# Decode attention kernel: all transposes and scores of a tile first, then its softmax chain between parts of the value product of the tile before

## The chip, the cores and the metric

The kernel runs on one core of one Trainium2 chip. The metric is the device time of one execution in microseconds (us), medians of several runs.

## The reference

One decode step of attention with a cache, times a gate that a small MLP computes. What matters is the attention: 4 batches times 8 K/V heads, 8192 cached positions of 256 numbers in bf16, two query heads for each K/V head.

```python
B, Sq, D = 4, 1, 448
Hq, Hkv, Sk, Dh = 16, 8, 8192, 256
...
q = (x @ wq).reshape(B, Sq, Hq, Dh).transpose(0, 2, 1, 3)
k = repeat(k_cache, 2, axis=1); v = repeat(v_cache, 2, axis=1)
scores = einsum("bhqd,bhkd->bhqk", q, k) * (Dh ** -0.5)
o = einsum("bhqk,bhkd->bhqd", softmax(scores), v)
...            # output projection, times the gate, plus x
```

There are 32 pairs of batch and K/V head. The kernel calls each a tile (`h` = 0 to 31). A tile has 4 MiB of K and 4 MiB of V, each used once: 268 MB in all.

## The kernel before

K and V have two buffers each (`h % 2`). For each tile TensorE transposes K in 16 groups of 8 blocks (`f_t`); VectorE and ScalarE copy each group from PSUM to SBUF; TensorE multiplies it with the query (`f_s`, three groups behind: `LAG`). Then comes the softmax chain: row maxima (VectorE), their transpose on TensorE (`f_rmaxT`), global maximum (VectorE), broadcast by a matmul (`f_bc`), exponentials (ScalarE), sum by a matmul (`f_sum`). Last is the value product (`f_pv`, 128 matmuls).

```python
    J_RMAX, J_BC, J_SUM = 4, 6, 9
    PV_SLOTS = tuple(range(10, 16))
...
            def load_k(h):                       # issued by SyncE, K buffer free again
                if h >= 2:
                    sp.wait_ge(S["p_t"], NGR * (h - 1))
...
            def load_v(h):                       # V buffer free: value product of h-2 done
                    sp.wait_ge(S["p_pv"], h)
...
            for h in range(2, NH):
                load_k(h)
                load_v(h - 1)
            load_v(NH - 1)
...
            def body(h):                         # TensorE; NGR = 16
                for j in range(NGR):
                    f_t(h, j)
                    if j >= LAG:
                        f_s(h, j - LAG)
                    else:
                        f_s(h - 1, NGR + j - LAG)
                    if j == J_RMAX:
                        f_rmaxT(h - 1)
                    if j == J_BC:
                        f_bc(h - 1)
                    if j == J_SUM:
                        f_sum(h - 1)
                    if j in PV_SLOTS:
                        i, n = PV_SLOTS.index(j), len(PV_SLOTS)
                        f_pv(h - 1, NPV * i // n, NPV * (i + 1) // n)

            with nc.Fori(0, NH // 2, ...):       # a loop on TensorE: 2 bodies, 16 times
                body(0)
                body(1)

            h = NH - 1                           # after the last body
            for j in range(NGR - LAG, NGR):
                f_s(h, j)
...
            for g in range(0, 3):                # output product of 7 groups of heads,
                f_o(g)                           # with tile 31's chain between its parts
            f_rmaxT(h)
            for g in range(3, 6):
                f_o(g)
            f_bc(h)
            for g in range(6, HKV - 1):
                f_o(g)
            f_sum(h)
            # ... value product of tile 31 in four pieces, last group of the output product
```

So a body holds the last three score groups and the whole chain of the tile before it.

## Time and profile before

| | before |
|---|---|
| median time | 665.11 us (664.92 to 665.47, 3 runs) |
| loads | 279 MB, 431 GB/s from 40 to 640 us |
| TensorE idle until K is there | 93.9 us, 30 times |
| first transpose of the first tile, of the last tile | 31.26, 635.92 us |
| result stored from | 660.93 us |

The page of the profile. The rows of digits are 40 slices of the span, in tenths, 9 for 90% and more.

```profile
span 663.0 us, 27886 instructions
...
PE   2388887789888878987887898888888887789777
...
PEclk9997888898877899888789987878998788899889
DMA  8999999999999999999999999999999999999993
```

The DMA row is full from the second slice to the last but one. TensorE is not, and its granted clock is below full in most slices. The table of windows gives the busy time of each engine in a stretch, then clock, DMA share and GB/s:

```profile
40.00:640.00 600.00, 499.38 (x11974) 493.53 (x11972) 220.94 (x491) 235.04 (x336) 5.59 (x30) 0.87 1.01 431
...
635.00:641.00 6.00, 5.08 (x88) 5.09 (x89) 2.07 (x4) 2.05 (x2) 0.00 (x0) 0.72 0.98 422
...
650.00:652.00 2.00, 2.00 (x70) 2.00 (x67) 1.12 (x2) 0.24 (x1) 0.00 (x0) 1.00 0.66 274
652.00:654.00 2.00, 2.00 (x112) 1.75 (x112) 0.99 (x5) 0.00 (x0) 0.00 (x0) 1.00 0.12 49
```

The loads run without a gap until about 651 us and then stop. What follows is not bound by loads. The view of waits (in total, times, longest, in us) shows what TensorE stands idle for:

```profile
PE pst L484 <- PEq L436: 93.9, 30, 8.1
```

L484 is the transposes; the wait ends when the K of the tile has landed, 3 us per body. So the loop goes at the pace of the loads. The timeline of the end (start, duration, engine, line, operation, and in brackets the idle time before it):

```profile
635.92 0.61 PE L484 MATMUL pst<-ident_b,kn 128*128 128x128 bf16 x8 [3.11 <-PEq L436]
...
645.67 0.68 PE L522 MATMUL psv<-pT,vb 128*128 128x32 bf16 x21 [0.41 <-PEq L436]
...
655.90 0.36 PE L514 MATMUL psm<-rowsum,ones_f 128*128 128x2 f32 x2 [0.78 <-PEq L436]
...
660.93 0.63 SPq L160 DMA_DIRECT2D out_dram<-out_b  x2
```

The last K is there at 635.92 us, and from then TensorE needs 25.01 us to the store, with waits of 0.41 us (for the V of tile 30) and 0.78 us (for the exponentials of tile 31), and 0.42 us before the last group of the output product.

### The profile page before, as it was taken

The page shows a single profiled execution, that of the slowest core. Times are in us where ns is not written, and L with a number is a line of the kernel's source. Part 1 is how long each engine was busy: PE and PEld are TensorE (multiplying, and loading weights), DVE is VectorE, ACT ScalarE, POOL GpSimd, SP SyncE. Part 2 cuts the span into 40 slices and gives each one's busy share as a digit, 9 for nine tenths or more (in the row PEclk, how much of TensorE's full clock was granted, in tenths as well). Part 3 has the DMA queues.
Part 4 walks back from the last instruction along what each step waited for, and adds up shares of the span by engine and source line. Part 5 has one row for each costly group of instructions (what it writes and reads, how often), then busy time and mean ns, then how long its engine had stood idle before and what let it go on. Part 6 is the DMA issues. An engine that isn't in the chain of part 4 may idle for free. (4 is left out here: it accounts for less than half of the span.)

```text
span 663.0 us, 27886 instructions
## 1 busy us (share of the span) xinstructions
PE 534.6 (81%) x12964; PEld 527.5 (80%) x12964; DVE 247.4 (37%) x583; ACT 250.0 (38%) x362; POOL 12.1 (2%) x45
## 2 busy tenths in 40 slices
PE   2388887789888878987887898888888887789777
PEld 2388887789888878987887898888888887789777
DVE  6233433333333333333333333433343333334332
ACT  1044433344433344444333444433444343344431
POOL 3000000000000000000000000000000000000000
PEclk9997888898877899888789987878998788899889
DMA  8999999999999999999999999999999999999993
GB/s 354 439 403 427 429 439 425 431 437 429 429 433 431 431 433 431 433 431 429 435 429 429 439 425 431 441 423 431 439 427 429 437 431 427 437 431 427 433 418 132
DMA packets 14379, 279.24 MB, mean 421 GB/s; under 512 B 1172, under 2 KB 5272, under 8 KB 5528
## 3 DMA queue, kind: packets, MB, share of 16 engines
q1 hardware_dynamic: 14344, 279.00, 98.3%
q8 instruction: 11, 0.18, 0.1%
q14 instruction: 8, 0.07, 0.0%
q10 hardware_dynamic: 16, 0.00, 0.0%
HBM read 278.99 MB, written 0.00 MB: 421 GB/s over the span
## 5 line engine op out<-in xcount | busy, mean ns | idle before, releaser
L484 PE MATMUL pst<-ident_b,kn 128*128 128x128 bf16 x4096 | 364.0, 241 | 95.5 <-PEq L436 93.9
L241 ACT ACTIVATE kT<-pst 128x1024 bf16<-128x1024 bf16 x224 | 226.8, 1023 | 366.8 <-PE pst L484 366.7
L484 PEld LDWEIGHTS pst<-ident_b,kn 128*128 128x128 bf16 x4096 | 279.2, 108 | 98.9 <-issue 97.5
L239 DVE COPY kT<-pst 128x1024 bf16<-128x1024 bf16 x288 | 199.3, 692 | 392.1 <-PE pst L484 392.1
L496 PE MATMUL psc<-qc,kT 128*128 128x2 bf16 x4120 | 182.8, 166 | 0.3 <-issue 0.3
L496 PEld LDWEIGHTS psc<-qc,kT 128*128 128x128 bf16 x4120 | 170.5, 101 | 1.3 <-issue 1.3
L522 PE MATMUL psv<-pT,vb 128*128 128x32 bf16 x4096 | 132.4, 177 | 13.3 <-PEq L436 9.1
L522 PEld LDWEIGHTS psv<-pT,vb 128*128 128x128 bf16 x4096 | 116.7, 96 | 14.6 <-issue 14.6
L261 ACT ACTIVATE pT<-psc,negb 128x64 bf16<-128x64 f32 x66 | 20.8, 330 | 18.5 <-DVE negb L391 18.5
L232 POOL COPY qc<-qT 128x4 bf16<-128x4 bf16 x32 | 6.0, 186 | 607.2 <-PE psc L496 597.2
L261 ACT ACTIVATION_READ_ACCUMULATOR pT<-psc,negb 128x1 f32 x66 | 12.9, 196 | 0.0
L514 PE MATMUL psm<-rowsum,ones_f 128*128 128x2 f32 x66 | 12.0, 251 | 0.8 <-PEq L436 0.8
L509 PE MATMUL psm<-diag,ones_f 2*128 2x2 f32 x66 | 12.5, 256 | 0.0
L442 PE MATMUL pst<-ident_b,xn_b 4*128 4x4 bf16 x14 | 0.6, 161 | 12.8 <-DVE xn_b L309 8.1
L442 PEld LDWEIGHTS pst<-ident_b,xn_b 4*128 4x128 bf16 x14 | 0.5, 99 | 12.8 <-issue 8.1
L514 PEld LDWEIGHTS psm<-rowsum,ones_f 128*128 128x128 f32 x66 | 9.9, 189 | 0.9 <-issue 0.9
L509 PEld LDWEIGHTS psm<-diag,ones_f 2*128 2x128 f32 x66 | 9.7, 183 | 0.8 <-issue 0.2
L403 DVE TENSOR_TENSOR OT<-psv,rz 128x2 bf16<-128x2 f32 x65 | 7.6, 162 | 7.1 <-PE psc L579 3.1
L505 PE MATMUL psm<-ident_f,rmax 128*2 128x128 f32 x33 | 9.9, 299 | 0.0
L379 DVE TENSOR_REDUCE rmax<-psc 128x2 f32<-128x128 f32 x33 | 9.3, 281 | 0.4 <-PE psc L496 0.4
L384 DVE TENSOR_REDUCE gmax<-psm 2x1 f32<-2x128 f32 x33 | 8.8, 268 | 0.6 <-PE psm L505 0.6
L386 DVE TENSOR_SCALAR diag<-ident_f,gmax 2x2 f32<-2x2 f32 x33 | 7.1, 216 | 1.2
(70 smaller groups left out, 66.8 us busy)
## 6 DMA issues: line engine op xcount, KB each, us to landing
kn<-in_A_k_cache_dram SPq DMA_DIRECT2D x32, 4096.0 KB, 23.1
vb<-in_A_v_cache_dram SPq DMA_DIRECT2D x31, 4096.0 KB, 32.1
vb<-in_A_v_cache_dram SPq DMA_DIRECT2D x4, 1024.0 KB, 18.3
vb<-in_A_wq_dram SPq DMA_DIRECT2D x1, 3584.0 KB, 11.2
wo_sb<-in_A_wo_dram SPq DMA_DIRECT2D x1, 3584.0 KB, 46.7
vb<-in_B_w_dram SPq DMA_DIRECT2D x2, 1568.0 KB, 16.9
out_dram<-out_b SPq DMA_DIRECT2D x2, 0.9 KB
out_dram<-out_b ACTq DMA_DIRECT2D x2, 0.9 KB
```

Source lines behind the costliest of these rows:

```text
L239: engine.tensor_copy(dst, src).then_inc(S["v_ev"], 1)
L241: engine.activation(dst, src, ACT.Copy).then_inc(S["a_ev"], 1)
L261: ins = act.activation(pv_p[:, :, hh], sc[:, :, hh], ACT.Exp, bias=negb[:, s, hh:hh + 1], scale=SCALE, accum_out=rowsum[:, s, hh:hh + 1])
L379: v.tensor_reduce(rmax[:, :], psc[h % 2][:, 0:NCH * REP].rearrange("p (k h) -> p h k", h=REP), AX.X, ALU.max).then_inc(S["v_rmax"], 1)
L384: c(v.tensor_reduce(gmax[:, :], psm[0:REP, 0:P], AX.X, ALU.max))
L403: ins = v.tensor_tensor(OT[:, g, :, dh, b], src[:, dh * PVW:dh * PVW + REP], rz[:, :], ALU.mult)
L484: ins = pe.transpose(dst[:, t * P:(t + 1) * P], kn[:, h % 2, GC * j + kl, half * P:(half + 1) * P], ident_b[:, :])
L496: ins = pe.matmul(psc[h % 2][:, kk * REP:(kk + 1) * REP], kT[:, j % RING, t * P:(t + 1) * P], qc[:, h % 2, half, :], start=(half == 0), st ...
L505: pe.transpose(psm[0:REP, 0:P], rmax[:, :], ident_f[:, :]).then_inc(S["p_m1"], 1)
L509: pe.matmul(psm[:, P:P + REP], ones_f[0:REP, :], diag[:, :], start=True, stop=True).then_inc(S["p_m2"], 1)
L514: pe.matmul(psm[:, P + REP:P + 2 * REP], ones_f[:, :], rowsum[:, h % 2, :], start=True, stop=True).then_inc(S["p_m3"], 1)
L522: ins = pe.matmul(psv[:, dh * PVW:(dh + 1) * PVW], vb[:, h % 2, kk, dh * P:(dh + 1) * P], pT[:, h % 2, kk * REP:kk * REP + PVW], start=(kk ...
```

## The change

It makes a body work on one tile: all transposes with the scores behind them, then the last three score groups and the three small matmuls of the chain, each after a part of the value product of the preceding tile, which is to cover the chain's latency. K's buffer comes free earlier in the body. The dummy scores of a tile before the first go away, and with them some memsets. `rz` gets two buffers because it now lives longer.

```diff
-    J_RMAX, J_BC, J_SUM = 4, 6, 9
-    PV_SLOTS = tuple(range(10, 16))
+    PV_PARTS = (0, 12, 24, 44, 72, 100, NPV)
...
                     f_t(h, j)
                     if j >= LAG:
                         f_s(h, j - LAG)
-                    else:
-                        f_s(h - 1, NGR + j - LAG)
-                    if j == J_RMAX:
-                        f_rmaxT(h - 1)
-                    if j == J_BC:
-                        f_bc(h - 1)
-                    if j == J_SUM:
-                        f_sum(h - 1)
-                    if j in PV_SLOTS:
-                        ...
+                tail = [lambda j=j: f_s(h, j) for j in range(NGR - LAG, NGR)]
+                tail += [lambda: f_rmaxT(h), lambda: f_bc(h), lambda: f_sum(h)]
+                for i, f in enumerate(tail):
+                    f_pv(h - 1, PV_PARTS[i], PV_PARTS[i + 1])
+                    f()
...
             h = NH - 1
-            for j in range(NGR - LAG, NGR):
-                f_s(h, j)
             take("dwo", 16)
-            for g in range(0, 3):
+            take("v_ot")
+            for g in range(HKV - 1):
                 f_o(g)
-            f_rmaxT(h)
-            ...                     # chain of tile 31 between the groups
-            f_sum(h)
... # VectorE, ScalarE: chain after a tile's copies; semaphore counts one lower
```

## The prediction

> **What bounds the kernel now.** The loads. The table of windows (20 us each) shows the DMA share at 0.99 to 1.06 and 416 to 439 GB/s in every window from 40 to 640 us. [...]Each loop body (one tile) needs one 4 MiB K and one 4 MiB V: the K issues of the SP queue from 71.39 to 612.68 us are 28 periods of 19.33 us, 434 GB/s. TensorE has slack: the waits view shows 93.9 us in 30 waits until K lands, 3 us per body. K lands 23.1 us and V 32.1 us after issue, so over 10 us are always queued.

> Only the end is not set by loads. DMA throughput dies at about 651.3 us (274 GB/s in 650 to 652, 49 after), but the result is ready at 660.9. The last K lands at about 635.9; TensorE then works 25 us, almost without a gap.

> **What the change does.** Same matmuls, less three dummy score groups. The softmax chain of a tile moves from the next body into its own, between parts of the preceding tile's value product. K's buffer is free some 5 us earlier in a body, V's at the end as before. The order of loads is unchanged.

> *Steady state, TensorE warm:* a transpose group issues in 0.41 us, a score group in 0.24, 21 value matmuls in 0.53 (timeline, 646 to 652). All transposes and 13 score groups: 16*0.41 + 13*0.24 = 9.7 us. Tail: value product 3.2, three score groups 0.7, three small matmuls 0.7, and waits: rmax transpose to broadcast took 0.96 us at the end of before, with 0.8 of work to cover it; broadcast to sum 1.43, with 1.0: about 0.6 us exposed. Body about 15 us. TensorE idles before each K, and its clock falls to 0.5 afterwards ([...]the trace shows 0.50 for 5 to 6 us after a 3 us gap). A cold start adds about 2 us: 17, still under 19.33. The new waits come out of slack: gain of the loop, 0.

> *End:* after the last K lands, before does also the last three score groups and the chain of tile 30 (1.1 + 0.7 us), waits 0.4 us for V, and waits about 1.1 us in the chain of tile 31. With the change only tile 31's chain is left, 0.6 us exposed. Estimate: 9.7 + 2 (cold) + 5.3 + output product of seven groups 1.5 + 4.9 (measured from the last value product to the result) = 23.4 us against 25.0; warm, 21.4. I take 2 us saved.

> *Start:* bound by the first K's landing (31 us): 0.

> **Prediction: 663.0 us, 80% range 659.5 to 666.0.** Chances: faster by over 2% 0.02, within 2% 0.95, slower by over 2% 0.03.

> **What would show it.** DMA share 1.0 and 430 GB/s from 40 to 640 us again; K issues 19.3 us apart; K's time to landing up from 23 to about 28 us, V's down from 32 to about 29; short new TensorE waits (0.2 to 0.5 us) before the broadcast and sum matmuls, 15 to 25 us in total, idle before the first transpose still 2 to 4.5 us; last K at about 636 us and result 21 to 24 us later.

> **What would make it wrong.** Bodies above 19.33 us: if the clock stays halved longer[...], or copies of transposed tiles stall the dense transpose phase, TensorE becomes the limit, +3% or more. Or a load queue running empty: DMA share below 0.95.

What no trace of this case showed is cut from it, as marked. Its sum for the end: 23.4 us from the last K to the result, 21.4 at full clock.

## More of the kernel before

The experiments ran in three sessions on three chips. The kernel before ran in each of them, with medians of 665.41 to 665.44 us; so between sessions the ratios are to be compared.

## The result and the profile after

The kernel after takes 663.86 us (663.70 to 664.02, 4 runs) against 665.29 us (664.92 to 665.75, 4 runs). The ratio is 0.9978, 95% interval 0.9961 to 0.9995. All ratios here are the mean time of one kernel's fast runs over that of the kernel before in the same rounds, so not quite the ratios of the medians quoted. The gain of 1.4 us is small but outside the interval.

The page:

```profile
span 661.7 us, 27809 instructions
...
PE   2397898879888889988878987888898888889787
...
PEclk9998687898778798877879887779987877998779
DMA  8999999999999999999999999999999999999994
```

The windows:

```profile
40.00:640.00 600.00, 509.20 (x11964) 501.65 (x11962) 231.36 (x493) 240.80 (x339) 5.59 (x30) 0.85 1.01 431
...
635.00:641.00 6.00, 5.18 (x62) 5.21 (x63) 1.89 (x3) 2.05 (x2) 0.00 (x0) 0.50 0.96 414
...
650.00:652.00 2.00, 1.98 (x66) 1.88 (x63) 0.67 (x4) 0.19 (x1) 0.00 (x0) 1.00 0.67 283
652.00:654.00 2.00, 1.53 (x86) 1.40 (x85) 0.41 (x3) 0.51 (x4) 0.00 (x0) 1.00 0.13 53
```

The loads are as before, 431 GB/s, and stop at the same moment. TensorE's clock is lower (0.85 against 0.87 over the loop), and at the start of the last tile it is half for the whole window. The waits:

```profile
PE pst L468 <- PEq L420: 82.2, 30, 8.1
...
PE psm L497 <- PEq L420: 8.5, 31, 0.3
...
PE psm L492 <- PEq L420: 2.9, 1, 2.9
```

The wait for K shrank by 12 us and short waits for the sum (L497) took 8.5 us, in 31 of the 32 bodies. The waits for V before the value product fell from 9.1 us in 18 bodies to 2.4 us once. At the lower clock TensorE was busy for 10 us more from 40 to 640 us. The end:

```profile
635.82 3.57 PE L468 MATMUL pst<-ident_b,kn 128*128 128x128 bf16 x32 [2.65 <-PEq L420]
...
652.66 0.35 PE L497 MATMUL psm<-rowsum,ones_f 128*128 128x2 f32 x2 [0.28 <-PEq L420]
...
653.20 1.55 PE L536 MATMUL pst<-wo_sb,OT 128*4 128x112 bf16 x112 [0.19 <-PEq L420]
...
659.52 0.63 SPq L159 DMA_DIRECT2D out_dram<-out_b  x2
```

First transposes start at 31.20 us (31.26 before) and those of the last tile at 635.82 us (635.92 before). So 31 tiles take 604.62 us against 604.66: start and loop changed nothing. From the last K to the store it is 23.70 us against 25.01. The gain is at the end.

### The profile page after: what moved, and what is told of

The parts are those of the page before. It is cut to its first block, busy times and chain, and to the rows that moved or that the text cites. A ratio compares the mean times of both kernels' runs of the same rounds, so it can differ in the third digit from the quotient of the medians.

```text
span 661.7 us, 27809 instructions
## 1 busy us (share of the span) xinstructions
PE 543.9 (82%) x12935; PEld 535.4 (81%) x12935; DVE 256.4 (39%) x577; ACT 255.1 (39%) x358; POOL 9.5 (1%) x44
## 5 line engine op out<-in xcount | busy, mean ns | idle before, releaser
L468 PE MATMUL pst<-ident_b,kn 128*128 128x128 bf16 x4096 | 356.1, 245 | 82.4 <-PEq L420 82.2
L468 PEld LDWEIGHTS pst<-ident_b,kn 128*128 128x128 bf16 x4096 | 289.0, 111 | 84.5 <-issue 84.4
L239 ACT ACTIVATE kT<-pst 128x1024 bf16<-128x1024 bf16 x224 | 229.2, 1023 | 233.9 <-PE pst L468 233.9
L480 PE MATMUL psc<-qc,kT 128*128 128x2 bf16 x4096 | 177.1, 164 | 1.0 <-issue 1.0
L480 PEld LDWEIGHTS psc<-qc,kT 128*128 128x128 bf16 x4096 | 157.8, 98 | 1.1 <-issue 1.1
L497 PE MATMUL psm<-rowsum,ones_f 128*128 128x2 f32 x64 | 11.8, 253 | 8.5 <-PEq L420 8.5
L497 PEld LDWEIGHTS psm<-rowsum,ones_f 128*128 128x128 f32 x64 | 9.9, 195 | 10.8 <-issue 10.8
L383 DVE COPY negb<-psm 128x2 f32<-128x2 f32 x32 | 5.1, 159 | 20.4 <-PE psm L492 20.4
L387 DVE RECIPROCAL rz<-psm 128x2 f32<-128x2 f32 x32 | 5.5, 170 | 12.7 <-PE psm L497 12.7
## 6 DMA issues: line engine op xcount, KB each, us to landing
kn<-in_A_k_cache_dram SPq DMA_DIRECT2D x32, 4096.0 KB, 27.1
vb<-in_A_v_cache_dram SPq DMA_DIRECT2D x31, 4096.0 KB, 32.2
```

Of the source, the lines that this page charges most:

```text
L239: engine.activation(dst, src, ACT.Copy).then_inc(S["a_ev"], 1)
L468: ins = pe.transpose(dst[:, t * P:(t + 1) * P], kn[:, h % 2, GC * j + kl, half * P:(half + 1) * P], ident_b[:, :])
L480: ins = pe.matmul(psc[h % 2][:, kk * REP:(kk + 1) * REP], kT[:, j % RING, t * P:(t + 1) * P], qc[:, h % 2, half, :], start=(half == 0), st ...
L497: pe.matmul(psm[:, P + REP:P + 2 * REP], ones_f[:, :], rowsum[:, h % 2, :], start=True, stop=True).then_inc(S["p_m3"], 1)
```

## The experiments

Theory A: start and loop are bound by the loads, so the change moves only slack there; the 1.4 us come from the end, where after the last K there is less to do and to wait for. Rival B: the deeper queue of loads makes the loads faster. A second question is what the change does to TensorE's own time, which the loads hide.

### e1: K issued as late as before

```diff
                 if h >= 2:
                     sp.wait_ge(S["p_t"], NGR * (h - 1))
+                    sp.wait_ge(S["p_pv"], h - 1)
```

> The kernel after, but each K load waits also for the value product before it, so it is issued when it was before the change. Theory A (only the end of the kernel got shorter; the loop is bound by the loads either way): time as after, 1.4 us under before (ratio 0.998), K to landing back to 23 us. Rival B (the deeper queue of loads makes the loads a little faster): the gain goes, ratio 1.000.

Measured: 664.16 us, ratio 0.9989 (0.9976 to 1.0002). K's time to landing fell from 27.1 to 22.5 us. The interval holds both expectations, so the ratio doesn't decide. The record also has the span of every execution, the time between the first and the last instruction on the core. Time and span differ by 1.8 to 2.1 us in most executions, but by 3.0 us in the slowest one of e1 (665.74 us, span 662.7). The mean span is 662.26 us for e1 (5 executions) against 663.50 for before in the same rounds (11): 1.24 us less, with an estimated standard error of 0.2 from their spread. So most of the gain is still there without the deeper queue. The trace of this kernel stores its result at the same 659.52 us as the kernel after:

```profile
636.22 3.57 PE L469 MATMUL pst<-ident_b,kn 128*128 128x128 bf16 x32 [3.08 <-PEq L421]
...
659.52 0.63 SPq L159 DMA_DIRECT2D out_dram<-out_b  x2
```

That the two are equal to the hundredth is chance: the last tile starts 0.40 us later here and its dense phase (first transpose to first value matmul) is 0.44 us shorter, with less of it at half clock (8 transposes take 0.61 us again from 640.69 us on, in after from 641.37). Rival B is refuted as the main cause; a part of some 0.4 us for the queue (the mean span of after is 661.85 us, in another session) is not excluded.

### e2 and e3: the end alone, and the end undone

e2 is the kernel before with only the last body in the new form; e3 is the kernel after with only the last tile's chain put back. Both need the last two bodies written out after the loop:

```diff
-            with nc.Fori(0, NH // 2, ...):
+            with nc.Fori(0, NH // 2 - 1, ...):
                 body(0)
                 body(1)
+            body(0)
+            body(1, last=True)
```

> The kernel before with the loop unchanged for 31 tiles, and only the last tile's softmax chain put between parts of the value product of tile 30, as the change does. Theory A: most of the gain is here, since the waits of the tail (0.41 for V, 0.17 and 0.92 in the chain) turn into 0.28 and 0.19: about 1.0 us under before (ratio 0.9985), last K's landing at the same time, result about 24.0 us after it instead of 25.0. Rival B or a gain in the loop or the start: ratio 1.000.

> The kernel after, with only the last tile's chain put back between the groups of the output product, as before. Theory A: about 0.6 us slower than after, 0.8 us under before (ratio 0.9988), result about 24.3 us after the last K landed. Rival B: as after (0.998).

Measured: 670.72 us (1.0081) and 670.66 us (1.0084). Both miss, upwards, and the trace shows a reason apart from the chain. In the written-out bodies of e2 TensorE stops for 1 to 2 us at a time, where the profile shows nothing that it waits for:

```profile
634.81 0.47 PE L526 MATMUL psv<-pT,vb 128*128 128x32 bf16 x12 [2.10 <-issue]
...
641.24 0.30 PE L499 MATMUL psc<-qc,kT 128*128 128x2 bf16 x6 [1.69 <-issue]
...
648.89 0.16 PE L499 MATMUL psc<-qc,kT 128*128 128x2 bf16 x1 [2.00 <-issue]
```

The instruction queue of the DMA view has 17 packets (e3: 17 too) instead of 11 (before) and 10 (after). The packed trace, the stored records behind the profile, has the times of these packets: in the kernel after none comes between 76 and 655 us, in e2 eight come from 626.3 us on (e3: from 626.1), and each of the three waits above ends 2.4 to 2.6 us after one of them (632.3, 638.8, 646.3). That TensorE waited for these packets was not shown; it is my reading of their times. So e2 and e3 decide nothing on the end.

### e4 and e7: keeping TensorE's clock up

The last tile's dense phase (first transpose to first value matmul) took 635.82 to 647.84 = 12.0 us, the first 5 us of it at half clock. e4 fills the idle time at the end of each body with 56 unused matmuls of 128 columns; e7 with 14 of 512.

```diff
                     f_pv(h - 1, PV_PARTS[i], PV_PARTS[i + 1])
                     f()
+                for _ in range(NWARM):      # e4: 56 with 128 columns; e7: 14 with 512
+                    pe.matmul(pst[0][:, :], ident_b[:, :], kT[:, 0, 0:512], start=True, stop=True)
```

> The kernel after with 56 unused 128-column matmuls (about 3.1 us) at the end of each body, in the idle time before K, to keep the TensorE clock up. If half a clock at the start of the last body costs what the trace says (its dense phase took 12.0 us against 9.7 with a full clock), the result comes 21.4 us after the last K instead of 23.7, and the time is 2.3 us under after: 661.6 us (ratio 0.9944). The other 31 bodies get faster by as much and give it all back as idle time. If the clock falls in spite of it, or the bodies exceed 19.3 us, no gain or a loss.

> The idea of e4_warm with a quarter of the instructions: 14 unused matmuls of 512 columns (about 3 us) per body. If e4 was slow [...](83 instruction packets of 16 KB instead of 10), this loop has 10 or 11 packets, no long issue waits, and is 2.3 us under after: 661.6 us (ratio to before 0.9944). If e4 was slow because of the busy TensorE itself (3 us more work per body, clock, or a later free buffer), this is as slow: 740 us or more.

e4 took 767.04 us (1.1493), a hundred more. Its DMA view has, for the instruction queue:

```profile
q8 instruction: 83, 1.36, 0.7%
```

and its timeline has issue waits in most tiles, such as

```profile
286.30 0.56 PE L507 MATMUL psv<-pT,vb 128*128 128x32 bf16 x14 [3.51 <-issue]
...
314.21 1.12 PE L524 MATMUL pst<-ident_b 128*128 128x128 bf16 x17 [1.71 <-issue]
```

83 packets of 16 KB against 10. In the packed trace the packets come in groups of nine, a group about every 89 us, which is two rounds of the loop; the waits come with them (286.30 above, then at 375.70, 464.17, 553.43). By the program a body has 389 matmuls, each with a weight load (the page of before counts 12,964 of both); two bodies are 1,556 such instructions, with e4's addition 1,780, with e7's 1,612. What a group of packets brings in, and why the longer loop draws them and the shorter ones do not, the traces do not show; instructions for semaphores were not counted. e7 (same idea, a quarter of the unused instructions) shows that the number of added instructions is the cause and not the busier TensorE: TensorE is busy for 550 us from 40 to 640 us (e4: 511), yet there are 11 packets, issue waits of over 0.3 us only in the first bodies and once (0.54 us) after the loop, 664.98 us (1.0000). The issue waits of value product, scores and unused matmuls in e4 sum to 50 us (30.6, 11.9 and 7.5 in the view of waits); the other 50 I did not follow up, beyond that its loads fell to 380 GB/s from 40 to 640 us.

e7 did not reach its own expectation of 661.6 us either. The reason is in the last tile:

```profile
636.10 1.95 PE L469 MATMUL pst<-ident_b,kn 128*128 128x128 bf16 x32 [1.47 <-PEq L421]
...
645.85 0.45 PE L507 MATMUL psv<-pT,vb 128*128 128x32 bf16 x12
...
651.09 2.97 PE L524 MATMUL pst<-kT,ident_b 128*128 128x512 bf16 x13
```

The dense phase now takes 9.75 us instead of 12.0, as expected, but the unused matmuls stand also behind the last tile, where nothing is idle, and cost 2.9 us on the critical path. That was my mistake in placing them.

### e5 and e6: half of the loads

To see TensorE's own pace, both kernels load only half of each K and V and use each block twice. This computes something else. (The comparison with the reference still passed, so its tolerance does not notice such a change in this data; it is no evidence of correctness here.)

```diff
-                sp.dma_start(kn_dst(h), A_k_cache[b, g]...)
+                sp.dma_start(kn[:, h % 2, 0:NCH // 2, :]..., A_k_cache[b, g]...[:, 0:NCH // 2, :]...)
...
-                                       kn[:, h % 2, GC * j + kl, ...
+                                       kn[:, h % 2, (GC * j + kl) // 2, ...
... # V and the value product likewise
```

> Wrong result on purpose: the kernel before with half of every K and V loaded, each loaded block used twice, so that TensorE and not the loads limit the loop. Body from the trace's issue times: 16 * 0.65 us for transposes and scores, 3.2 for the value product, 0.7 for small matmuls: 14.3 us with no waits; about 31 + 32 * 14.3 + 12 = 500 us.

> The same for the kernel after. If the waits that the change adds are real and only hidden by the loads (0.28 before the sum, 0.1 before the broadcast, the empty pipeline at the start of each dense phase), the body takes 15.0 us and this kernel is 15 to 25 us slower than e5_half_before. If the new order helps TensorE as was perhaps meant (longer runs of the same work, fewer waits), it is as fast or faster.

Measured: 506.91 us for before, 538.26 us for after, ratios 0.7619 and 0.8079 in the same rounds. So the change costs 31 us, 6%, once TensorE is the limit, more than I expected. From 24 periods of K issues a body takes 14.31 us before and 15.38 after. The timeline of e6 shows several kinds of bodies:

```profile
251.11 0.35 PE L498 MATMUL psm<-rowsum,ones_f 128*128 128x2 f32 x2 [0.28 <-PEq L421]
251.63 3.53 PE L469 MATMUL pst<-ident_b,kn 128*128 128x128 bf16 x32 [0.16 <-PEq L421]
267.78 0.35 PE L498 MATMUL psm<-rowsum,ones_f 128*128 128x2 f32 x2 [0.28 <-PEq L421]
282.56 0.35 PE L498 MATMUL psm<-rowsum,ones_f 128*128 128x2 f32 x2 [0.28 <-PEq L421]
283.08 1.95 PE L469 MATMUL pst<-ident_b,kn 128*128 128x128 bf16 x32 [0.16 <-PEq L421]
```

The body from 267.78 to 282.56 takes 14.78 us: 0.47 more than before, of which 0.28 is the wait before the sum, its only one. Every second body also has the wait of 0.16 us before its first transposes. The one from 251.11 takes 16.67, mostly because 32 transposes took 3.53 us instead of 1.95. In half-microsecond windows the granted clock is 0.50 from 252 to 255 us there, and full for the rest of 240 to 286 us. Two waits of less than half a microsecond together, in a loop that is otherwise never idle, were followed here by some 3.5 us of half clock, but not each time: from 90 us on in 8 of the 14 bodies that have both waits. The body from 282.56 has both, keeps its clock and takes 15.09 us.

### e8: each K in four pieces

```diff
+                wk = NCH // 4
+                for i in range(4):
+                    sp.dma_start(kn[:, h % 2, i * wk:(i + 1) * wk, :]..., src[:, i * wk:(i + 1) * wk, :]...
+                                 ).then_inc(S["dk%d%d" % (h % 2, i)], 16)
...
-                if j == 0:
+                if j % 4 == 0:       # wait for the piece
```

> The kernel after with each K loaded in four pieces with a semaphore each, so that the transposes of the last tile start when its first piece is there and not when the last is. Last tile's first transpose at about 633 us instead of 635.9; then TensorE waits for the last but one V (lands at about 645.6): result at 657.3 us of the profile (full clock then) to 659.5 (half clock after that wait), so 661.7 to 663.9 us. If the pieces make the loads slower, 665 us or more.

Measured: 670.71 us (1.0079), the third of the outcomes named. The loads got slower. From 100 to 600 us, this kernel:

```profile
100.00:600.00 500.00, 414.21 (x9895) 407.06 (x9896) 189.79 (x408) 196.34 (x279) 4.88 (x26) 0.79 1.01 427
```

against 432 GB/s in the same window before and after. By the end the V of tile 30 lets the value product start at 653.09 us instead of 645.67 (before). Here K in pieces of 1 MiB (8 KB per partition), with V still in 4 MiB (32 KB per partition), lost 1.2% against 4 MiB for both, with the DMA engines as busy (share 1.01 against 1.00). In a kernel that is bound by loads that is 7 us (670.71 against 663.86). Whether it is the size, the shorter rows or the number of transfers is not shown.

### e9 and e10: unused matmuls ahead of the wait for K, in both kernels

```diff
             def body(h):
+                for _ in range(NWARM):      # 17; GpSimd clears this part of kT at the start
+                    pe.matmul(pst[0][:, :], ident_b[:, :], kT[:, 0, 0:512], start=True, stop=True)
                 for j in range(NGR):
```

> The kernel after with 17 unused matmuls of 512 columns (3.7 us) at the start of each body, ahead of the wait for K, so that none is left behind the last tile (in e7 13 of them, 2.9 us, stood between the last body and the output product, and an issue wait of 0.5 us in the last value product). First transpose of the last tile at about 636.0 us as before, its dense phase 9.75 us as in e7 instead of 12.0, result 21.4 to 21.7 us after the landing: 657.5 us of the profile, 661.7 us (ratio to before 0.9945). If TensorE's clock had nothing to do with the end, 664 us.

> The same 17 matmuls in the kernel before. If the change's gain at the end was 2 us of work and waits as predicted, less about 0.6 because its last body happens to run at half clock for longer (5 us against 3.5), then with a full clock in both the difference between this kernel and e9 is 2.0 us or more: about 663.7 us (ratio 0.9975). If the clock plays no part in the difference, it stays at 1.4 us.

e9, the change with its clock kept up, takes 662.51 us (0.9955, 0.9942 to 0.9968), the fastest of all. Its end:

```profile
636.20 1.95 PE L470 MATMUL pst<-ident_b,kn 128*128 128x128 bf16 x32 [0.81 <-PEq L422]
...
655.35 0.33 PE L553 MATMUL psv<-pT,vb 128*128 128x32 bf16 x7 [0.57 <-issue]
...
658.46 0.63 SPq L160 DMA_DIRECT2D out_dram<-out_b  x2
```

22.26 us from the last K to the store, 0.57 of it an issue wait. The expectation was 21.4 to 21.7. The dense phase takes 9.75 us as in e7 (granted clock 1.00 from 635 to 650 us).

e10, the same in the kernel before, takes 666.90 us (664.93 to 668.59; 1.0024, 1.0010 to 1.0039): not faster than the kernel before but a little slower, and my 663.7 is missed. The change does gain more here, 4.4 us between the medians and not 2, but this kernel did not get the full clock at its end, which the expectation had supposed. The trace, of an execution of 665.70 us, shows why:

```profile
645.56 0.70 PE L524 MATMUL psv<-pT,vb 128*128 128x32 bf16 x21 [1.34 <-PEq L438]
646.10 1.01 PE L486 MATMUL pst<-ident_b,kn 128*128 128x128 bf16 x8
```

With the full clock (1.00 from 630 to 640 us) TensorE comes to its first value matmul earlier and then waits for V, which lands no sooner than before (645.56 against 645.67). In the old order five more groups of transposes and their scores stand behind that wait. The first two of them run at half clock after it (1.01 us for 8 transposes instead of 0.61; granted clock 0.83 from 640 to 650 us). In the new order V is not needed until every transpose is done. The waits for V sum to 25.7 us in 24 bodies here, against 9.1 in the kernel before. What made the slower executions (up to 668.59 us) slower still was not traced.

### e11: a longer wait in every body

```diff
-    PV_PARTS = (0, 12, 24, 44, 72, 100, NPV)
+    PV_PARTS = (0, 12, 24, 44, 100, NPV - 1, NPV)
```

> The kernel after with 27 of the 28 value matmuls before the sum moved ahead of the broadcast, so that the wait for the exponentials is about 0.7 us longer in each of 32 bodies. Theory A (waits in the loop are paid out of slack, only the last body counts): K issues still 19.4 us apart, time under 1 us above after: 664.6 us (ratio to before 0.9988). If waits in the loop count, 32 * 0.7 = 22 us more: 686 us.

Measured: 665.15 us (1.0003, 0.9990 to 1.0016). The waits for the sum are 30.5 us in all instead of 8.5, and the waits for K are 57.9 us instead of 82.2. The last tile's first transpose starts at 635.96 us, 0.14 later than after. So 22 us of added waits in the loop cost nothing: this is theory A's main claim, shown. The end is 1.65 us later than after, more than the 0.7 I allowed:

```profile
653.20 0.35 PE L497 MATMUL psm<-rowsum,ones_f 128*128 128x2 f32 x2 [0.95 <-PEq L420]
653.73 2.61 PE L536 MATMUL pst<-wo_sb,OT 128*4 128x112 bf16 x112 [0.18 <-PEq L420]
...
661.17 0.63 SPq L159 DMA_DIRECT2D out_dram<-out_b  x2
```

0.67 is the longer wait; 1.06 is the output product, 2.61 us instead of 1.55: the granted clock is 0.50 from 654.0 to 657.0 us, after that wait. Of the rest, the last tile starts 0.14 later and its dense phase is 0.30 shorter.

## Why the prediction was right

**The loads bound the loop, so the loop gains nothing.** Right: 604.62 us for 31 tiles against 604.66, 431 GB/s in both. The experiments show it from both sides: half the loads take 158 us off the kernel before, and 22 us of added waits in e11 leave the last tile where it was.

**The body needs about 15 us warm and 17 cold, under the period of the loads.** Right: 14.78 us warm in e6 (15.09 with the second wait), dense phase 12.0 us cold against 9.75 warm. I took the period as 19.33 us from the K issues; between first and last transposes it is 19.5, which changes nothing.

**New waits of 0.6 us per body, 15 to 25 us in total.** Too large: 0.28 us before the sum in each body, 8.5 us, and 2.9 us once before a broadcast (11.4 together). It was harmless because slack pays for it.

**K's time to landing up to 28 us, V's down to 29.** K's went to 27.1. V's did not move (32.1 to 32.2): I put its issue at the moment the next K lands, while the body still ends some 3 us before that, as it did.

**The end gains 2 us.** The mechanism is right and the size a little off: 1.31 us after the last K, 1.43 between the medians. The sum in the prediction, 23.4 us with the cold start, was nearly met (23.70); taking 2 instead of the 1.6 which it gives was the mis-sized step, leaning to the warm case (21.4), which did not happen. An account from the two timelines, as an estimate: three score groups and the chain of tile 30 no longer in the last body, 3 * 0.24 + 0.65 = 1.4 us less; waits of 0.28 + 0.19 instead of 0.41 + 0.78, 0.7 less; but half clock for longer, which costs 12.0 - 9.75 = 2.3 us against 1.35 before (four groups in 3.95 us instead of 4 * 0.65), 0.9 more. Together 1.2 of 1.3 us. e9 shows what the clock costs: kept up, the dense phase is 2.27 us shorter and the median 1.35 us lower (in another session; the ratio goes from 0.9978 to 0.9955).

What stays open: e2 and e3, which were to show the end by itself, were spoiled by issue waits (1 to 2 us each in e2, next to 17 instruction packets), so the split of the 1.3 us rests on the traces and on e9 to e11. The clock at the last tile is partly luck. The packed traces list each stretch at half clock. From 85 us to the last tile it lasts 3.4 or 6.8 us: 6.8 us in 12 of 29 stretches before and in 20 of 29 after. The last tile drew 3.4 us (from 636.7) before and 6.8 us (from 634.2) after; the traces of e1 and e11, which have the new order, also have 6.8 there, with dense phases of 11.58 and 11.72 us. So the longer stretch is the usual one after the change and not the only one; how much the gain varies with it from execution to execution was not traced.

## What to carry to other kernels

In a loop bound by loads, look for a gain only before the first transfer and after the last: follow the chain from the last landing to the store, and count what stands behind each late input (in e11, 22 us of added waits in the loop moved the last tile by 0.14 us). A reordering that looks free there may still cost TensorE time (6% here once the loads were halved), so test it with the loads cut before you keep it for a case where they are not the limit. When TensorE is at half clock just ahead of the critical end, as here (0.50 from 635 to 641 us in after), a few large unused matmuls ahead of the wait can help (1.35 us in e9), if they don't stand behind the last tile (2.9 us in e7), don't bring the instruction packets and issue waits of e4 (83 packets, 100 us more), and if no later input then becomes the wait (1.34 us for V in e10).
